# An RWKV-5 attention with a gated mixture of experts: 96 instead of 128 rows loaded per item, and half of the decayed r of six items moved from GpSimd to VectorE

## The chip, the cores and the metric

The kernel runs on one core of one Trainium2 chip. The core has five engines that run their own instruction streams: TensorE (PE, with weight loads listed as PEld), VectorE (DVE), ScalarE (ACT), GpSimd (POOL) and SyncE (SP, which here only issues transfers). 16 DMA engines move data between HBM and the on-chip memory. The metric is the device time of one execution in microseconds; 377.44 us is the median of three runs of the kernel before (376.11 to 377.89).

## The reference

Two blocks in a row. The attention keeps a 48 by 48 state per batch and head, decayed by `w` at each of 768 steps; the second block routes each token to one of eight experts.

```python
B, H, S, D = 4, 8, 768, 48
for t in range(S):
    cur = einsum('bhd,bhe->bhde', u * k[:, :, t], v[:, :, t])
    y[:, :, t] = einsum('bhd,bhde->bhe', r[:, :, t], state + cur)
    state = w[:, :, None] * state + einsum('bhd,bhe->bhde', k[:, :, t], v[:, :, t])
x = y, heads side by side            # (4, 768, 384)
e = argmax(x @ w_gate), or the expert of the token before where sigmoid(x @ w_local) >= 0.5
out = softmax(x @ w_gate)[e] * (relu(x @ w1[e]) @ w2[e])   # 8 experts, 384 -> 1024 -> 384
```

## The kernel before

**Items.** The attention runs over 16 items, one per batch and pair of heads, item n in `Attention.run`'s loop of 17 turns. An item's two heads lie on rows (partitions) 0 to 47 and 64 to 111 of a 128-row tile; rows 48 to 63 and 112 to 127 are zeros that the host put into the arrays. The 768 steps are cut into 6 chunks (`NCH`) of 128. Inside a chunk the recurrence becomes matrix products; between chunks a state is carried.

**Loads.** `load(n)` issues three transfers on SP: rk (r and k by feature, 1536 numbers a row; item 0's in two parts), kv (k and v by token) and vT (v by feature, 768 numbers a row). There are four buffers for rk and for vT (`AHEAD`) and five for kv, and `load(n + 3)` stands at the head of turn n. Eight semaphores serve these transfers in turn, so that each waits until the eighth before it has landed.

**Steps of an item.** With the lines of the profile:

- POOL, `scale(n)`, one turn ahead of PE: pd = r times k (L217, two halves of 384), ke = k by token with the decays to the chunk's end (L213), rw = r times powers of w (`decayed`, L230, two halves, for n above 2). The order is rw, ke, pd except for the first items (pd, ke) and item 4 (ke, rw, pd).
- DVE, `keys(n)`: kw = k times the inverse powers of w (L237; in two halves for items 0 to 2). For items 0 to 2 DVE makes rw as well, interleaved with kw, from a copy of the powers (`first`) that ACT puts into PSUM tile mp; `inv`, kw's factor, is also in PSUM. `reciprocals(i)` (L156, L157) makes `inv` of head pair i by a Newton step on DVE.
- PE: scores of kw and rw (L291, two groups into two PSUM banks, `pair`), which DVE masks into am (L293, two of 768); own (L268), the u term from pd, which DVE multiplies with vT (L276, y); added (L249), the chunk sums from ke and v into mp, which DVE's scan turns into the states S (L255); inside (L300), am times v; before (L313), rw times S; then ACT copies y out (L321), PE turns it (L332) and ACT stores it into x (L334). After the last item of a batch come the logits (L345, L346, L351, L352).

The banks `pair` alternate: every score group, turn or logits product takes the other one and has to wait until its last reader is done.

**Order.** The Tile framework runs with a manual schedule: each engine takes its instructions in the order in which the program is written, and `run` is that order. In turns 1 and 2 PE does scores, own and added of item n behind inside and before of item n − 1. From turn 4 on the scores run one item ahead, and kw two items ahead of that turn (turn 4 makes kw of items 4, 5 and 6, turn n makes that of n + 2). From turn 5 on DVE's order in a turn is: first am, y, kw, second am, scan.

**Constants.** `__init__` builds `tab`, a table of the powers of w and of 1/w (L121 to L132; head pair 0 on DVE, the rest on POOL), and `step`, factors for the scan (L117). `warm` and `align` are PE transposes without a use of their result. The router behind the attention needs iotas from POOL (`numbering`, in turn 2) and casts of them from ACT (`cast`, in turn 6); its own steps lie between the attention's on DVE, such as L709, L741 and L806. Expert 0's weights are fetched in the last turns, and from about 110 us on the experts run, which the change does not touch.

## Time and profile before

| | |
|---|---|
| median of three runs | 377.44 us |
| the profiled execution | 379.17 us |
| its span, first to last instruction | 377.5 us |
| mean granted TensorE clock | 0.996 |
| busy: PE, DVE, ACT, POOL | 363.0, 247.7, 110.3, 148.7 us |
| read from HBM | 64.79 MB |

The profile's page gives each engine's busy time, then the span in 40 slices of 9.4 us: a digit is the busy share of a slice in tenths, and the row DMA is the mean share of the 16 DMA engines. A row of the timeline has start, duration, engine, source line, operation, output and inputs, shape, count (neighbours of one kind are merged, so that x2 with 1.82 us are two operations), and in brackets how long the engine stood idle before and what ended that idle time. In the list of groups a row ends with the group's busy time and the mean ns of one. Times of PE operations overlap, because matmuls are pipelined; a busy PE may be waiting inside. "Issue" stands for time in which nothing shown was waited for. Where the engine named as the end of a wait had long been done, the wait was for something else, often a transfer.

### The profile page before, as it was taken

How to read it: one execution, taken by the hardware profiler on the slowest of the kernel's cores; microseconds unless marked ns; L12 is line 12 of the kernel's file. 1: busy time of each engine (PE TensorE's matmuls, PEld its weight loads, DVE VectorE, ACT ScalarE, POOL GpSimd, SP SyncE). 2: the span in 40 equal slices, each digit the busy share in tenths (PEclk: the TensorE clock that was granted, in tenths of full speed). 3: DMA queues.
4: the chain of work that ended last, by engine and by line, in shares of the span. 5: the costliest groups of instructions: out<-in, count | busy, mean ns of one | idle time of the engine just before them, and what ended most of it. 6: DMA issues, size and time to landing. Idle time of an engine off the chain costs nothing. (4 is left out here: it accounts for less than half of the span.)

```text
span 377.5 us, 9676 instructions
## 1 busy us (share of the span) xinstructions
PE 363.0 (96%) x3844; PEld 319.6 (85%) x3844; DVE 247.7 (66%) x718; ACT 110.3 (29%) x304; POOL 148.7 (39%) x207
## 2 busy tenths in 40 slices
PE   7899999999989999999999999999999999999992
PEld 6676777786769998999899999999999998989971
DVE  6988778888834835787557656857767767555300
ACT  4132233233532211322332233333243233331210
POOL 7689999786222055212333113313233023021012
PEclk9999999999999999999999999999999999999998
DMA  7999999983669457713352452164165065162011
GB/s 245 417 411 410 407 405 338 370 300 109 196 232 340 160 188 296 299 27 115 140 198 62 147 214 87 49 218 190 38 207 213 22 215 206 21 257 112 2 41 38
DMA packets 17765, 74.93 MB, mean 199 GB/s; under 512 B 2778, under 2 KB 6624, under 8 KB 15408
## 3 DMA queue, kind: packets, MB, share of 16 engines
q1 hardware_dynamic: 10336, 56.89, 40.7%
q0 software_dynamic: 3424, 9.48, 7.4%
q10 hardware_dynamic: 3952, 7.87, 5.7%
q8 instruction: 32, 0.52, 0.6%
q14 instruction: 21, 0.17, 0.1%
HBM read 64.79 MB, written 9.47 MB: 197 GB/s over the span
## 5 line engine op out<-in xcount | busy, mean ns | idle before, releaser
L1333 POOL DMA_INDIRECT out_dram<-yo,sid x27 | 26.6, 985 | 115.5 <-ACT yo L1328 92.0
L1184 PE MATMUL h<-exT,w1t 128*128 128x168 f32 (+4 forms) x240 | 54.9, 327 | 0.0
L1188 DVE TENSOR_TENSOR hT<-h,hs 128x168 f32<-128x168 f32 (+3 forms) x60 | 21.1, 351 | 46.1 <-PE h L1184 29.6
L1107 POOL DMA_INDIRECT xg<-x_d,gid x29 | 31.1, 1072 | 34.1 <-DVE gid L877 15.1
L1184 PEld LDWEIGHTS h<-exT,w1t 128*128 128x128 f32 x240 | 41.6, 190 | 0.3 <-issue 0.3
L1134 PE MATMUL h<-exT,w1t 128*128 128x168 f32 (+2 forms) x192 | 37.2, 333 | 0.5 <-DVE lt L698 0.5
L1253 PE MATMUL y<-factors,sums 128*128 128x192 f32 x168 | 36.8, 326 | 0.0
L293 DVE TENSOR_TENSOR am<-pair,kept 128x768 f32<-128x768 f32 x32 | 30.0, 953 | 8.9 <-PE pair L291 8.4
L217 POOL TENSOR_TENSOR pd<-rk 128x384 f32<-128x384 f32 x32 | 31.5, 1006 | 10.6 <-PE y L268 10.0
L1184 PE MATMUL h<-xs,ws 128*128 128x168 f32 (+4 forms) x144 | 35.3, 327 | 0.0
L1134 PEld LDWEIGHTS h<-exT,w1t 128*128 128x128 f32 x192 | 30.9, 190 | 2.6 <-DVE lt L698 0.6
L1184 PEld LDWEIGHTS h<-xs,ws 128*128 128x128 f32 x144 | 25.5, 190 | 4.3 <-ACT hs L1191 1.2
L1253 PEld LDWEIGHTS y<-factors,sums 128*128 128x128 f32 x168 | 28.9, 190 | 0.2
L291 PE MATMUL pair<-rw,kw 48*64 48x128 f32 (+1 forms) x768 | 23.4, 249 | 1.9 <-issue 1.1
L300 PE MATMUL y<-am,kv 128*64 128x128 f32 x360 | 22.9, 276 | 1.3 <-DVE y L276 1.2
L230 POOL TENSOR_TENSOR rw<-rk,tab 128x384 f32<-128x384 f32 x26 | 23.7, 936 | 0.4 <-DMA rk<-in_rk_dram 0.4
L1121 DVE COPY exT<-tp 128x384 f32<-128x384 f32 (+5 forms) x29 | 13.9, 485 | 14.7 <-PE tp L1120 14.6
L291 PEld LDWEIGHTS pair<-rw,kw 48*64 48x64 f32 x768 | 19.6, 133 | 4.6 <-issue 2.8
L1253 PE MATMUL y<-w2t,hT 128*128 128x192 f32 x96 | 23.0, 328 | 0.0
L213 POOL TENSOR_TENSOR ke<-kv,endT 128x288 f32<-128x288 f32 (+1 forms) x32 | 21.9, 705 | 1.9 <-DMA kv<-in_kv_dram 1.0
L321 ACT COPY xT<-y 128x768 f32<-128x768 f32 x15 | 12.0, 800 | 33.1 <-PE y L313 31.1
L300 PEld LDWEIGHTS y<-am,kv 128*64 128x64 f32 x360 | 19.4, 137 | 2.4 <-DVE y L276 1.7
(298 smaller groups left out, 736.6 us busy)
## 6 DMA issues: line engine op xcount, KB each, us to landing
w1t<-in_w_dram SPq DMA_DIRECT2D x8, 1536.0 KB, 6.9
w2t<-in_w_dram SPq DMA_DIRECT2D x8, 1536.0 KB
rk<-in_rk_dram SPq DMA_DIRECT2D x15, 768.0 KB, 8.4
kv<-in_kv_dram SPq DMA_DIRECT2D x16, 584.0 KB, 7.1
vT<-in_vT_dram SPq DMA_DIRECT2D x16, 384.0 KB
x_d<-x ACTq DMA_DIRECT2D x4, 1152.0 KB
w1t<-in_w_dram SPq DMA_DIRECT2D x2, 768.0 KB
w2t<-in_w_dram SPq DMA_DIRECT2D x2, 768.0 KB
```

The costliest lines, as they stand in the source:

```text
L213: nc.gpsimd.tensor_mul(t["ke"][:, z], t["k"][:, z], spread(self.endT[:, p, hp], 1, len(range(NCH)[z])))
L217: nc.gpsimd.tensor_mul(t["pd"][:, z], t["rT"][:, z], t["kT"][:, z])
L230: engine.tensor_mul(t["rw"][:, z], t["rT"][:, z], spread(pw, 1, z.stop - z.start))
L291: nc.tensor.matmul(sc[f * DP:(f + 1) * DP, h, i, x:], lhsT=t["kw"][q, c, o * DP:(o + 1) * DP], rhs=t["rw"][q, c, x:], start=True, stop=True)
L293: return lambda: nc.vector.tensor_mul(t["am"][:, g], sc, spread(self.kept[:, g:g + 3], 1, 2))
L300: nc.tensor.matmul(t["y"][h][p * DP:(p + 1) * DP, c2 * P:(c2 + 1) * P], lhsT=t["v"][:, (2 * c + h) * DH:(2 * c + h) * DH + DP], rhs=t["am" ...
L1107: self.nc.gpsimd.indirect_dma_start(out=xg[:n], out_offset=None, in_=self.x_d[:rows], in_offset=bass.IndirectOffsetOnAxis(ap=u["gid"][:n, ...
L1134: nc.tensor.matmul(h[:, :n], lhsT=u["w1"][:, m, kk, :], rhs=u["xT"][:, kk, :], start=(kk == 0), stop=(kk == DK - 1))
L1184: nc.tensor.matmul(out, lhsT=a, rhs=b, start=start and k == 0, stop=stop and k == len(terms) - 1, skip_group_check=True)
L1188: nc.vector.tensor_tensor(out, a, b, op=Alu.add)
L1253: return lambda: nc.tensor.matmul(bank[:, x * half:(x + 1) * half], lhsT=a, rhs=b, start=(j == 0 and x == 0), stop=(j == FK // 2 - 1), ski ...
L1333: self.nc.gpsimd.indirect_dma_start(out=out.rearrange("n (h d) -> (n h) d", h=2) if half else out, out_offset=bass.IndirectOffsetOnAxis(ap ...
```

## The change

1. **Loads.** rk comes as two transfers of 48 rows (0 to 47 and 64 to 111) for all items but 0 and 3, and vT likewise for all but items 0, 2 and 3. The zeros in the other rows stay in a buffer from one item to the next. Buffers that get no whole load first are cleared on the chip: rk buffer 1 by a DVE memset, vT buffer 1 and rk buffer 2 by three ACT copies of 768 zeros from step. These stand ahead of the loads in the program. For item 4 kv is issued ahead of rk.
2. **Decayed r.** For items 3 to 8 POOL makes the first half of rw and DVE the second, behind kw, with the factor from tab in SBUF. For item 2 DVE makes the first half and POOL the second.
3. **Reciprocals of head pair 1.** `inverse(1)`, three operations on POOL and an ACT copy into `inv`, takes the place of `reciprocals(1)` on DVE, and the three warming transposes ahead of it on PE go.
4. **Numbering.** The iotas move from turn 2 to turn 8, ahead of `scale(9)`, and the casts from turn 6 to turn 8.

```diff
+SHARED = range(3, 9)
...
+        self.step = once.tile([P, HP, DH, NCH - 1], F32, name="step")
+        nc.vector.memset(self.step, 0.0)
+        nc.vector.memset(self.rks[1], 0.0)
+        zero = self.step.rearrange("p i d c -> p (i d c)")[:, :NCH * P]
+        for t in (self.vTs[1], self.rks[2]):
+            t = t.rearrange("p a c t -> p (a c t)")
+            for x in range(0, t.shape[1], NCH * P):
+                nc.scalar.copy(t[:, x:x + NCH * P], zero)
         for i in range(AHEAD - 1):
             self.load(i)
...
+    def inverse(self, i):
+        nc, w, inv = self.nc, self.tab[:, i, 0, 1:], self.tab[:, i, 1, 1:]
+        nc.gpsimd.tensor_mul(self.more, w, inv)
+        nc.gpsimd.tensor_scalar(self.more, self.more, -1.0, 2.0, Alu.mult, Alu.add)
+        nc.gpsimd.tensor_mul(self.more, self.more, inv)
+        nc.scalar.copy(self.inv[:, i], self.more)
...
+        whole, parts = (slice(0, P),), (slice(0, DH), slice(DP, DP + DH))
+        rows = whole if n in (0, AHEAD - 1) else parts
+        src = self.rk_d[b, hp].rearrange("p (a c t) -> p a c t", a=2, c=NCH)
+        if n == AHEAD:
+            nc.sync.dma_start(out=kv, in_=self.kv_d[b, hp])
+        for z in (slice(0, NCH),) if n else (slice(0, C2), slice(C2, NCH)):
+            for q in rows:
+                nc.sync.dma_start(out=rk[q, :, z], in_=src[q, :, z])
+        if n != AHEAD:
+            nc.sync.dma_start(out=kv, in_=self.kv_d[b, hp])
+        for q in whole if n < AHEAD and n != 1 else parts:
+            nc.sync.dma_start(out=vT[q].rearrange("p a c t -> p (a c t)"), in_=self.vT_d[b, hp][q])
...
         def rw(i):
-            self.decayed(nc.gpsimd, n, slice(i * C2, (i + 1) * C2))
+            if i == 0 or n not in SHARED:
+                self.decayed(nc.gpsimd, n, slice(i * C2, (i + 1) * C2))
+        if n == 2:
+            rw(1)
...
-        pw = self.first[:, :P] if n < 3 else self.tab[:, t["hp"], 0, :P]
+        pw = self.first[:, :P] if n < 3 and engine is self.nc.vector else self.tab[:, t["hp"], 0, :P]
...
-            if n < 3:
+            if n < 2 or n == 2 and z.start == 0:
                 self.decayed(nc.vector, n, z)
+        if n in SHARED:
+            self.decayed(nc.vector, n, slice(C2, NCH))
...
-                self.warm(3)
+                self.inverse(1)
                 self.added(0)
-                self.reciprocals(1)
                 self.states(0)
                 self.scale(1)
...
-                else:
-                    router.numbering()
...
+            if n == HP * 2:
+                router.numbering()
             if n + 1 < M:
                 self.scale(n + 1)
...
-            if n == 6:
+            if n == HP * 2:
                 router.cast()
```

How the streams move, at the places that the prediction speaks of. First DVE from the powers of item 3 to the first am of item 5 in the program before (rk_160 is the buffer of item 3, rk_157 that of item 4, rk_158 that of item 5; tab and mp hold the powers):

```order
L157 SCALAR_TENSOR_TENSOR inv<-mp,tab 128x128
L237 TENSOR_TENSOR kw<-rk_160,inv 128x768
L660 MEMSET r_ones 128x128
L255 SCALAR_TENSOR_TENSOR S<-step,mp 128x240
L293 TENSOR_TENSOR am<-pair_152,kept 128x768
L293 TENSOR_TENSOR am<-pair_151,kept 128x768
L276 TENSOR_TENSOR y<-y,vT_164 128x2x384
L237 TENSOR_TENSOR kw<-rk_157,inv 128x768
L255 SCALAR_TENSOR_TENSOR S<-step,mp 128x240
L237 TENSOR_TENSOR kw<-rk_158,inv 128x768
L293 TENSOR_TENSOR am<-pair_151,kept 128x768
```

And the same stretch of DVE in the changed program:

```order
L265 TENSOR_TENSOR kw<-rk_160,inv 128x768
L257 TENSOR_TENSOR rw<-rk_160,tab 128x384
L689 MEMSET r_ones 128x128
L285 SCALAR_TENSOR_TENSOR S<-step,mp 128x240
L323 TENSOR_TENSOR am<-pair_151,kept 128x768
L323 TENSOR_TENSOR am<-pair_152,kept 128x768
L306 TENSOR_TENSOR y<-y,vT_164 128x2x384
L265 TENSOR_TENSOR kw<-rk_157,inv 128x768
L257 TENSOR_TENSOR rw<-rk_157,tab 128x384
L285 SCALAR_TENSOR_TENSOR S<-step,mp 128x240
L265 TENSOR_TENSOR kw<-rk_158,inv 128x768
L257 TENSOR_TENSOR rw<-rk_158,tab 128x384
```

One rw of 384 stands behind each kw: one ahead of the scan of item 3, two ahead of am of item 4.

POOL in the same part of the program before, from the last two of the iotas of `numbering` to pd of item 4 (rk_157; kv_168 and kv_169 hold items 3 and 4):

```order
L636 IOTA tie_i 128x6
L636 IOTA ief_i 1x8
L230 TENSOR_TENSOR rw<-rk_160,tab 128x384 x2
L213 TENSOR_TENSOR ke<-kv_168,endT 128x3x96
L213 TENSOR_TENSOR ke<-kv_168,endT 128x2x96
L217 TENSOR_TENSOR pd<-rk_160 128x384 x2
L213 TENSOR_TENSOR ke<-kv_169,endT 128x3x96
L213 TENSOR_TENSOR ke<-kv_169,endT 128x2x96
L230 TENSOR_TENSOR rw<-rk_157,tab 128x384 x2
L217 TENSOR_TENSOR pd<-rk_157 128x384 x2
```

And in the changed program, from the end of item 2's ke to the same pd:

```order
L232 TENSOR_TENSOR ke<-kv_167,endT 128x2x96
L257 TENSOR_TENSOR rw<-rk_160,tab 128x384
L232 TENSOR_TENSOR ke<-kv_168,endT 128x3x96
L232 TENSOR_TENSOR ke<-kv_168,endT 128x2x96
L236 TENSOR_TENSOR pd<-rk_160 128x384 x2
L232 TENSOR_TENSOR ke<-kv_169,endT 128x3x96
L232 TENSOR_TENSOR ke<-kv_169,endT 128x2x96
L257 TENSOR_TENSOR rw<-rk_157,tab 128x384
L236 TENSOR_TENSOR pd<-rk_157 128x384 x2
```

The iotas are gone from here and rw is one half instead of two. On DVE around item 7 (rk_160 now holds item 7) the rows between y of item 5 and the scan read, changed:

```order
L323 TENSOR_TENSOR am<-pair_151,kept 128x768
L306 TENSOR_TENSOR y<-y,vT_162 128x2x384
L265 TENSOR_TENSOR kw<-rk_160,inv 128x768
L257 TENSOR_TENSOR rw<-rk_160,tab 128x384
L323 TENSOR_TENSOR am<-pair_152,kept 128x768
L285 SCALAR_TENSOR_TENSOR S<-step,mp 128x240
```

Before, kw is followed by the second am there.

More of the change, by code (lines that the diff above doesn't have):

```diff
@@ L113, in __init__ @@
         nc.sync.dma_start(out=self.wp, in_=wp_d)
-        self.step = once.tile([P, HP, DH, NCH - 1], F32, name="step")
-        nc.vector.memset(self.step, 0.0)
         self.tab = tab = once.tile([P, HP, 2, P + 1], F32, name="tab")
@@ L133, in __init__ @@
             n += m
+        self.more = once.tile([P, P], F32, name="more")
         self.first, self.newton = mp[:, :P + 1], mp[:, P + 1:2 * P + 1]
@@ L192, in load @@
         rk, vT, kv = self.rks[n % AHEAD], self.vTs[n % AHEAD], self.kvs[n % (AHEAD + 1)]
-        if n:
-            nc.sync.dma_start(out=rk.rearrange("p a c t -> p (a c t)"), in_=self.rk_d[b, hp])
-        else:
-            for z in (slice(0, C2), slice(C2, NCH)):
-                nc.sync.dma_start(out=rk[:, :, z], in_=self.rk_d[b, hp].rearrange("p (a c t) -> p a c t", a=2, c=NCH)[:, :, z])
-        nc.sync.dma_start(out=kv, in_=self.kv_d[b, hp])
-        nc.sync.dma_start(out=vT.rearrange("p a c t -> p (a c t)"), in_=self.vT_d[b, hp])
+        whole, parts = (slice(0, P),), (slice(0, DH), slice(DP, DP + DH))
[10 more added lines that the diff above has]
+            nc.sync.dma_start(out=vT[q].rearrange("p a c t -> p (a c t)"), in_=self.vT_d[b, hp][q])
         self.items[n].update(b=b, hp=hp, rT=rk[:, 0], kT=rk[:, 1], vT=vT,
@@ L207, in scale @@
         t["pd"] = self.two.tile([P, NCH, P], F32, name="pd")
-        t["rw"] = self.four.tile([P, NCH, P], F32, name="rw")
+        self.room(n)
         hp = t["hp"]
@@ L225, in scale, with room @@
                 what(i)
+    def room(self, n):
+        t = self.items[n]
+        if "rw" not in t:
+            t["rw"] = self.four.tile([P, NCH, P], F32, name="rw")
     def decayed(self, engine, n, z):
         t = self.items[n]
-        pw = self.first[:, :P] if n < 3 else self.tab[:, t["hp"], 0, :P]
+        pw = self.first[:, :P] if n < 3 and engine is self.nc.vector else self.tab[:, t["hp"], 0, :P]
         engine.tensor_mul(t["rw"][:, z], t["rT"][:, z], spread(pw, 1, z.stop - z.start))
@@ L234, in keys @@
         t["kw"] = self.two.tile([P, NCH, P], F32, name="kw")
+        self.room(n)
         inv = self.inv[:, t["hp"]]
@@ L400, in run @@
                     self.reciprocals(2)
-                else:
-                    router.numbering()
                 self.scale(n + 1)
```

## The prediction

> **What bounds the kernel now.** I read the page first, then the busy time by stretches, then who waited for whom, then the timeline of the attention half. The page's span and slices (40 of 9.4 us):
>
> ```profile
> span 377.5 us, 9676 instructions
> ...
> DMA  7999999983669457713352452164165065162011
> GB/s 245 417 411 410 407 405 338 370 300 109 196 232 340 160 188 296 299 27 115 140 198 62 147 214 87 49 218 190 38 207 213 22 215 206 21 257 112 2 41 38
> ```
>
> The change touches only the attention half, up to about 110 us. There the DMA engines are full for six slices at about 410 GB/s, and the change takes bytes from them and work from GpSimd (POOL). But do these two set the pace? Two stretches by engine (columns PE, PEld, DVE, ACT, POOL, clock, DMA share, GB/s):
>
> ```profile
> 10.00:20.00 10.00, 8.95 (x191) 7.08 (x191) 9.11 (x17) 1.71 (x3) 7.04 (x9) 1.00 1.02 411
> 50.00:60.00 10.00, 9.98 (x238) 7.99 (x234) 7.71 (x10) 2.86 (x9) 9.34 (x12) 1.00 1.01 393
> ```
>
> Early, VectorE (DVE) is the fullest of the compute engines (9.11) and TensorE (PE) has gaps (8.95); later PE has none (9.98), and POOL at 9.34 looks as if it were short. Who waits for loads? In the table of waits up to 110 us (total, times, longest) only POOL waits for rk or kv, three times; two of the rows, and the third as it stands in the timeline:
>
> ```profile
> POOL ke L213 <- DMA kv<-in_kv_dram: 1.0, 1, 1.0
> POOL pd L217 <- DMA rk<-in_rk_dram: 0.4, 1, 0.4
> ```
>
> ```profile
> 21.37 1.69 POOL L230 TENSOR_TENSOR rw<-rk,tab 128x384 f32<-128x384 f32 x2 [0.42 <-DMA rk<-in_rk_dram]
> ```
>
> That is rw of item 3, and PE reads it 6 us later (the scan ahead of that item's am, quoted below, starts at 27.80). What PE waits for is DVE. Items 0 and 1, in order of time:
>
> ```profile
> 10.64 0.96 DVE L276 TENSOR_TENSOR y<-y,vT 128x768 f32<-128x768 f32 x1
> ...
> 10.87 0.49 PE L163 MATMUL pair<-ident 128*128 128x128 f32 x3
> ...
> 11.29 0.79 PE L249 MATMUL mp<-kv,ke 128*64 128x48 f32 x20
> ...
> 11.91 1.50 PE L300 MATMUL y<-am,kv 128*64 128x128 f32 x24
> 12.22 0.30 DVE L156 SCALAR_TENSOR_TENSOR mp<-mp,tab 128x128 f32<-128x128 f32 x1 [0.63 <-PE mp L249]
> ...
> 12.77 0.64 DVE L255 TENSOR_TENSOR_SCAN S<-step,mp 128x240 f32<-128x240 f32 x1
> 13.32 0.53 DVE L237 TENSOR_TENSOR kw<-rk,inv 128x384 f32<-128x384 f32 x1
> 13.46 0.90 PE L313 MATMUL y<-rw,S 48*48 48x128 f32 x20
> ...
> 13.77 0.55 DVE L230 TENSOR_TENSOR rw<-rk,mp 128x384 f32<-128x384 f32 x1
> ...
> 15.37 1.82 DVE L293 TENSOR_TENSOR am<-pair,kept 128x768 f32<-128x768 f32 x2
> 17.11 0.96 DVE L276 TENSOR_TENSOR y<-y,vT 128x768 f32<-128x768 f32 x1
> 18.12 1.53 PE L300 MATMUL y<-am,kv 128*64 128x128 f32 x24 [0.82 <-DVE y L276]
> ```
>
> So the first items are a chain PE scores, DVE am twice, DVE y, PE L300 and L313, PE scores; the last row says it, 0.82 of PE's idle time ended by y, and y stands directly behind am, am directly behind DVE's four kw and rw operations, which start 0.46 apart from 13.32 on. A load or a POOL operation that is done earlier does not shorten this chain; only what stands ahead of a link on DVE or PE does.
>
> **The start, and items 0 to 2.** Cost first: DVE clears rk buffer 1 (1536 elements a row) behind step, and ScalarE (ACT) writes zeros three times 768.
>
> ```profile
> 1.09 0.86 DVE L117 MEMSET step<- 128x960 f32 x1 [1.09 <-PEq L1770]
> 3.19 0.17 DVE L124 TENSOR_SCALAR w<-w_t 128x4 f32<-128x4 f32 x1 [1.23 <-DMA w_t<-in_wu_dram]
> 5.72 0.27 ACT L136 COPY mp<-tab 128x129 f32<-128x129 f32 x1 [3.13 <-DVE tab L132]
> ```
>
> 960 elements take 0.86 us, so 1536 take 1.37; DVE sat idle 1.23 us at that place, so the chain that starts at L124 is 0.14 late. ACT had 3.13 us free; three copies at about 0.8 (estimated from kw's 0.53 for 384 and am's 0.91 for 768) take 2.5 and cost nothing. The loads of items 1 and 2 wait for these writes, behind item 0's transfers that fill the DMA engines anyway.
>
> Gain: PE's three warming transposes (10.87 to 11.29) and DVE's two operations from 12.22 to 12.77 go. L300 of item 0 then starts when y is done: 10.64 + 0.96 + 0.14 + 0.05 = 11.79 instead of 11.91. The scan, which had ended at 13.41 and so held L313, can follow y and L249 at about 11.9 and be over at 12.6; L313 then stands behind L300's 1.50 alone, at 13.29 for 13.46: 0.17 gained on PE. DVE comes to kw of item 1 at about 12.6 for 13.32, 0.7 earlier. am needs both, the scores of PE and a free DVE, so L300 of item 1 gains between 0.17 and 0.7; I take 0.27, near PE's end, as DVE is now ahead. POOL's three operations in their stead (about 1.1 us by POOL's 0.94 for 384 elements and its start-up, between ke of item 0 and pd of item 1) lie under DVE's y and scan, and ACT's copy behind them under the scan; if POOL or ACT were over 0.3 late with them, kw would wait and the gain be gone. The half of item 2's rw that POOL makes instead of DVE gives nothing: from scores of item 2 on PE and am set the chain. **Sum so far −0.27 us.**
>
> The iotas move from behind item 2, where POOL waited 0.42 for rk afterwards, to behind pd of item 8, and ACT's casts with them to just ahead of the logits of that item. POOL's products are an item ahead there (below), so 0; if the casts held up ACT's copies, whose bank PE needs, it would be one cast group, at most 0.5 by ACT's 0.27 an operation.
>
> **Items 3 to 8: half of rw on DVE.** Six operations more, each 13.77 − 13.32 = 0.46 us of DVE. They differ from rw of items 0 to 2 in one point: the factor comes from tab in SBUF, not from mp in PSUM. What such a form costs beside POOL:
>
> ```profile
> 70.71 1.97 POOL L230 TENSOR_TENSOR rw<-rk,tab 128x384 f32<-128x384 f32 x2
> ...
> 71.81 0.89 DVE L709 SCALAR_TENSOR_TENSOR key<-lt,k 128x12 f32<-128x12 f32 x1
> ```
>
> ```profile
> L806 DVE SCALAR_TENSOR_TENSOR si<-r,eb 128x12 int32<-128x12 f32 x1 | 0.2, 172 | 0.0
> ```
>
> The same shape takes 0.17 us with POOL at rest and 0.89 here, ending at 72.70, when POOL's second half ends (72.68): a DVE operation with two SBUF inputs waits until POOL's running one is through. The wait lies between 0 and one POOL operation, 0.94:
>
> ```profile
> L230 POOL TENSOR_TENSOR rw<-rk,tab 128x384 f32<-128x384 f32 x26 | 23.7, 936 | 0.4 <-DMA rk<-in_rk_dram 0.4
> ```
>
> I take half of it times POOL's load after the change (about 0.8), 0.37. What DVE has to give, at the places concerned:
>
> ```profile
> 27.80 0.65 DVE L255 TENSOR_TENSOR_SCAN S<-step,mp 128x240 f32<-128x240 f32 x1 [0.70 <-PE mp L249]
> ...
> 34.66 1.82 DVE L293 TENSOR_TENSOR am<-pair,kept 128x768 f32<-128x768 f32 x2 [1.17 <-PE pair L291]
> ```
>
> Item 3: 0.46 + 0.37 against 0.70 of idle before the scan, 0.13 over. Items 4 and 5, both ahead of am of item 4: 1.66 against 1.17, 0.49 over; L345 and the scores of item 5 wait for that am's bank. Item 6 falls in a longer gap: 0. Items 7 and 8 stand between y and the second am, and PE's next scores need the bank that this am empties:
>
> ```profile
> 45.43 1.97 POOL L217 TENSOR_TENSOR pd<-rk 128x384 f32<-128x384 f32 x2
> 46.26 0.94 DVE L237 TENSOR_TENSOR kw<-rk,inv 128x768 f32<-128x768 f32 x1
> 47.12 0.95 DVE L293 TENSOR_TENSOR am<-pair,kept 128x768 f32<-128x768 f32 x1
> ...
> 48.43 0.28 PE L291 MATMUL pair<-rw,kw 48*64 48x128 f32 x2
> ...
> 52.44 0.95 DVE L293 TENSOR_TENSOR am<-pair,kept 128x768 f32<-128x768 f32 x1
> ...
> 53.89 0.27 PE L291 MATMUL pair<-rw,kw 48*64 48x128 f32 x2
> ```
>
> am ends at 48.07, the scores start at 48.43: 0.36 spare. For item 8 am ends at 53.39 and the scores start at 53.89: 0.50 spare. kw ends 0.20 before pd there, so the wait is 0.2: 0.66 − 0.36 = 0.30 and 0.66 − 0.50 = 0.16. **Sum 0.13 + 0.49 + 0.30 + 0.16 = +1.08.** With no wait at all only 0.10 stays; with 0.94 each time it is 0.70 + 1.63 + 1.04 + 0.90 = 4.27. POOL's lighter load itself buys nothing: pd of item 7 ends at 47.40, and PE reads it behind the scores of item 8, 6 us later.
>
> **The loads.** rk and vT now come as two transfers of 48 rows:
>
> ```profile
> rk<-in_rk_dram SPq DMA_DIRECT2D x15, 768.0 KB, 8.4
> kv<-in_kv_dram SPq DMA_DIRECT2D x16, 584.0 KB, 7.1
> vT<-in_vT_dram SPq DMA_DIRECT2D x16, 384.0 KB
> ```
>
> At 411 GB/s these take 1.91, 1.46 and 0.96 us, 4.33 an item. If time goes by bytes, an item's load falls to 0.75 × 2.87 + 1.46 = 3.61 and all comes earlier; as no DVE or PE operation waits for a load, that is worth 0. The trace of before has no load that covers part of the rows, so the other end is a rival below. [...]
>
> **Sum.** −0.27 + 1.08 + 0 = +0.8 us. The profiled execution took 379.17 us, its span 377.50 and 1.67 around it; the median of the three runs is 377.44, below it by 1.73, so I put the difference on both: 380.0 for such a profiled run, 378.2 for the median. About 0.5%, 1.9 us, is what a measurement of this kernel tells from no change.
>
> **Rivals.** *DVE's extra work is hidden* (15%): POOL, with half of rw gone, stands idle when DVE asks, and the waits are 0: −0.27 + 0.10, 377.3. For it: POOL waits for PE before later pd. Against: pd and kw start together, as quoted. *Faster* (13%): PE's early gaps are due to late data after all, through waits that the trace books on other engines, and earlier loads close them. From L313 of item 0 at 13.46 to the scores of item 8 at 53.89 are 40.4 us; six items at the pace of the last (53.89 − 48.43 = 5.46) would be 32.8. The other 7.6 hold one batch's logits, one set of scores made ahead, and the gaps of the first four items; if a third came back, it would be 2.4: 375.0. For it: DMA is full and POOL at 9.34 in this stretch. Against: the chain above names DVE and PE alone. *Slower through the loads* (19%): a transfer's time follows the rows at its fullest target, not its bytes. Point of decision, rk of item 5 for DVE's kw:
>
> ```profile
> 32.56 0.93 DVE L237 TENSOR_TENSOR kw<-rk,inv 128x768 f32<-128x768 f32 x1
> ...
> 95.48 0.94 DVE L237 TENSOR_TENSOR kw<-rk,inv 128x768 f32<-128x768 f32 x1
> ```
>
> At half speed, rk takes 2.88 and vT 1.44, 5.8 us an item. Before, the transfers up to rk of item 3 add up to 3 × 4.33 + 0.3 (wp) + 1.91 = 15.2, and POOL's wait for it ended at 21.37, 6.1 later. After, items 0 to 3 take 4.33 + 5.78 + 5.3 + 4.33 and 0.3 for wp, item 4 5.78 and rk of item 5 2.88: 28.7, landing at 34.8, 2.2 after 32.56. The idle 1.17 before am covers what the added rw leave of it, say 0.7: +1.5, with DVE's extra work 380. If each half takes as long as the whole, an item takes 7.2 us, the loads add up to 109, rk of item 15 lands at about 112 and kw wants it at 95.5: +16, 394. For it: no load of before covers part of the rows, so nothing rules it out. Against: 48 rows are fewer bytes, and every load of before ran at the rate of its bytes. [...]
>
> **How the numbers follow.** Forecast 50%, own range 377.3 to 381.4 (the two ends of DVE's wait). Hidden 15%, faster 13%, loads slower 19%, of which half about 380 and half about 394; 3% for what I have not seen. The range 375.3 to 381.4 leaves out the worst of the loads and a part of faster. Faster by over 0.5%: 13% and 2% of the rest. Slower: the forecast's upper part from 379.3 on (13%), and the loads' 17%. Same: 55%.
>
> **What would show it.** Right: L313 of item 1 near 19.3; the six new rw on DVE above 0.55 us where POOL runs, the am of item 4 at about 35 and a later scores row of items 7 and 8; rk landing earlier than before; POOL with gaps from 36 us on. Wrong: the new rw at 0.55 each, waits of DVE kw for rk, a DMA share still at 1.0 beyond 75 us, or L313 of item 4 well before 42.

## The result and the profile after

The changed kernel takes 401.81 us in the median of six runs (398.99 to 404.74), the kernel before 377.65 in six runs beside it (376.11 to 378.84): a ratio of 1.0634, 95% interval 1.0575 to 1.0692. That is 24 us slower, where +0.8 was forecast and the range ended at 381.4. The profiled execution of after (398.99, span 397.3) is the fastest of the six; against the span before it lost 19.8 us. Executions over 1.5% above the fastest of their kernel (one of 945 us in run 3, two in run 10, one in run 17) are left out of the times and ratios below.

The page of after, with the same lines as before and the granted clock (40 slices, now of 9.9 us):

```profile
span 397.3 us, 9734 instructions
...
PEclk9996996988899999999999999999999999999997
DMA  7999979979978665690345245146146145054011
GB/s 229 282 333 232 239 235 209 231 214 246 216 206 288 231 274 200 218 369 29 94 153 189 72 171 199 44 150 224 62 150 252 50 158 212 30 191 181 2 39 35
```

Read DMA and GB/s together. Before, the DMA engines were full for seven slices and moved 405 to 417 GB/s in the first five of them. Now they are full, or nearly, up to the thirteenth slice and from the fourth to the twelfth move 206 to 246. The program reads 4 MB less and the engines are busy for longer: that is no shortage of bytes but of rate. Two stretches, as shown of before, and one more (PE, PEld, DVE, ACT, POOL, clock, DMA share, GB/s):

```profile
10.00:20.00 10.00, 8.34 (x174) 6.35 (x168) 8.28 (x14) 1.92 (x4) 6.26 (x10) 1.00 1.02 284
...
50.00:60.00 10.00, 9.07 (x200) 7.29 (x196) 7.79 (x10) 2.49 (x6) 4.60 (x5) 1.00 0.76 232
60.00:70.00 10.00, 8.94 (x162) 7.18 (x164) 5.78 (x8) 1.64 (x4) 7.84 (x18) 0.66 1.04 209
```

From 50 to 70 PE had no gap before; now it has, and from 60 to 70 it is granted 0.66 of its clock. The waits up to 110 us name what was absent before (before, only POOL waited for rk or kv, three times, 0.4 to 1.0 us each):

```profile
POOL rw L257 <- DMA rk<-in_rk_dram: 12.5, 10, 2.6
POOL ke L232 <- DMA kv<-in_kv_dram: 9.0, 10, 1.7
DVE kw L265 <- DMA rk<-in_rk_dram: 2.9, 4, 1.3
```

The DMA queue of the loads, first before and then after (packets, MB, share of 16 engines over the span):

```profile
q1 hardware_dynamic: 10336, 56.89, 40.7%
```

```profile
q1 hardware_dynamic: 9904, 52.86, 44.8%
...
kv<-in_kv_dram SPq DMA_DIRECT2D x16, 584.0 KB, 10.7
rk<-in_rk_dram SPq DMA_DIRECT2D x28, 288.0 KB, 9.7
```

40.7% of 377.5 us are 153.6 us of the queue's time, 44.8% of 397.3 are 178.0: 24.4 us more for 4 MB less. The halves are 28 of rk (288 KB) and 26 of vT (144 KB), 12.1 MB; whole they would be 16.1 MB, 39.2 us at 411 GB/s. If all of the time more is put down to the halves, they took about 63.6 us, which is 190 GB/s, and a half of rk took 1.55 us where the whole one takes 1.91. This reckoning (queue time beyond 153.6 us) is used for each experiment below.

It charges the halves with more than their own time. The trace also has a record of every packet, and a packet's size tells its tensor: a row of rk has 6144 bytes, one of vT 3072, one of kv 4672. Mean times of a packet over items 4 to 15, and the queue's time for an item:

| | before | after |
|---|---|---|
| a row of rk | 249 ns | 460 ns |
| a row of vT | 136 ns | 201 ns |
| a row of kv | 184 ns | 300 ns |
| an item: rk + vT + kv | 1.99 + 1.09 + 1.47 = 4.55 us | 2.76 + 1.21 + 2.40 = 6.36 us |

kv comes whole, in 128 rows, in both kernels, and about half of the queue's extra time (12.6 us of the 24.4) is kv's. So a half is not only slow itself: the whole loads that stand in the queue with it become slow too. The rates of the reckoning are the price of such halves, not their own speed.

### The profile page after: what moved, and what is told of

The parts are those of the page before. It is cut to its first block, busy times and chain, and to the rows that moved or that the text cites. A ratio compares the mean times of both kernels' runs of the same rounds, so it can differ in the third digit from the quotient of the medians.

```text
span 397.3 us, 9734 instructions
## 1 busy us (share of the span) xinstructions
PE 375.4 (95%) x3841; PEld 327.6 (82%) x3841; DVE 254.1 (64%) x722; ACT 112.7 (28%) x308; POOL 145.8 (37%) x205
## 3 DMA queue, kind: packets, MB, share of 16 engines
q1 hardware_dynamic: 9904, 52.86, 44.8%
## 5 line engine op out<-in xcount | busy, mean ns | idle before, releaser
L257 POOL TENSOR_TENSOR rw<-rk,tab 128x384 f32<-128x384 f32 x21 | 19.2, 930 | 23.8 <-DMA rk<-in_rk_dram 13.6
L330 PE MATMUL y<-am,kv 128*64 128x128 f32 x360 | 27.0, 308 | 0.7 <-DVE y L306 0.7
L330 PEld LDWEIGHTS y<-am,kv 128*64 128x64 f32 x360 | 23.6, 159 | 1.7 <-DVE y L306 1.1
```

The lines of the kernel that those rows point to most:

```text
L257: engine.tensor_mul(t["rw"][:, z], t["rT"][:, z], spread(pw, 1, z.stop - z.start))
L330: nc.tensor.matmul(t["y"][h][p * DP:(p + 1) * DP, c2 * P:(c2 + 1) * P], lhsT=t["v"][:, (2 * c + h) * DH:(2 * c + h) * DH + DP], rhs=t["am" ...
```

## The experiments

Theories. **R**: a transfer of fewer rows is slow, and the loads set the pace. **N**: it is the number of transfers, five an item for three, on semaphore lanes that they share. **V**: VectorE's halves of rw. Ratios are against the kernel before, run beside each. The cuts of code show the loop over rk; vT is cut in the same way.

**1. Whole loads, the rest of the change kept.**

```diff
-        rows = whole if n in (0, AHEAD - 1) else parts
+        rows = whole
...
-        for q in whole if n < AHEAD and n != 1 else parts:
+        for q in whole:
```

> The changed kernel with every rk and vT loaded whole (128 rows, one transfer) again; the clears, the DVE halves of rw and the changed start stay. Theory R (rows: a transfer of 48 rows moves at about half the rate of one of 128, so the loads supply the attention too slowly): 378 to 379 us, DMA busy share down from 1.0 as in the kernel before, GB/s back to about 400 in the first 20 us. Theory N (number: five transfers an item instead of three, on eight shared lanes): also 378 to 379. Theory V (the loss is made by VectorE's halves of rw, which hold the pipeline up through the wait behind GpSimd): 395 to 402. This run also prices all of the change but its loads: my forecast of those parts was +0.8 us.

Measured: 378.19 us, ratio 0.9988 (0.9965 to 1.0011). The loss is gone with the halves, V falls, and all else in the change is worth −0.5 us (−1.3 to +0.4), where my steps gave +0.8.

```profile
DMA  7999999992669457713352452164165065072011
GB/s 244 415 411 410 405 389 317 343 368 90 206 239 356 154 191 307 289 39 124 121 198 62 164 215 70 54 229 178 37 208 217 16 218 204 20 260 111 3 42 36
```

Both rows are those of the kernel before again. The start, which the late loads hide in the changed kernel, can be read here: PE's L330 of item 1 and DVE's first kw of item 1 (18.12 and 13.32 in the rows of before):

```profile
17.70 1.53 PE L330 MATMUL y<-am,kv 128*64 128x128 f32 x24 [0.70 <-DVE y L306]
```

```profile
12.71 0.53 DVE L265 TENSOR_TENSOR kw<-rk,inv 128x384 f32<-128x384 f32 x1
```

**2. The loads and their clears alone, in the kernel before** (the changed `load` and the clears, nothing else).

> The kernel before with the change's loads and clears alone (48-row halves, VectorE's memset, ScalarE's clearing copies), no DVE halves of rw and the old start. Theories R and N: 397 to 402 us, granted clock near 0.96, GB/s 210 to 250 in the slices up to 120 us. Theory V: 376 to 380.

Measured: 400.44, ratio 1.0572 (1.0539 to 1.0605). With run 1 this closes the account: within the intervals the loads are all of the loss.

**3. and 4. The number of transfers against their shape.** Both keep five transfers an item and all bytes; one cuts rows, one cuts columns.

```diff
-            nc.sync.dma_start(out=rk.rearrange("p a c t -> p (a c t)"), in_=self.rk_d[b, hp])
+            for q in (slice(0, P),) if n == AHEAD - 1 else (slice(0, DP), slice(DP, P)):
+                nc.sync.dma_start(out=rk[q].rearrange("p a c t -> p (a c t)"), in_=self.rk_d[b, hp][q])
...
```

```diff
+            src, k = rk.rearrange("p a c t -> p (a c t)"), NCH * P
+            for z in (slice(0, 2 * k),) if n == AHEAD - 1 else (slice(0, k), slice(k, 2 * k)):
+                nc.sync.dma_start(out=src[:, z], in_=self.rk_d[b, hp][:, z])
...
```

> The kernel before with the same number of transfers as the change, but each half holds 64 rows (0 to 63, 64 to 127), so all of the bytes move (64.8 MB instead of 60.8). Theory R: slow, and slower than the change as the bytes are a third more per half: 400 to 420 us. Theory N: 397 to 404. If 48 rows are bad by their number (three rows for each of 16 DMA engines) and 64 are not: 377 to 380.

> The kernel before with the same number of transfers as the change, all bytes, but each rk and vT is cut by columns: two transfers of all 128 rows with half as many bytes in a row. Theory R: 377 to 380 us, GB/s as in the kernel before. Theory N: 397 to 404 us.

Measured: rows 413.03, ratio 1.091 (1.0874 to 1.0947); columns 377.78, ratio 0.9974 (0.9944 to 1.0005). GB/s by rows and by columns:

```profile
GB/s 226 226 315 224 220 276 195 242 233 206 246 265 313 279 250 218 213 291 271 32 172 141 126 39 180 200 41 184 205 36 240 164 102 249 36 165 194 2 38 34
```

```profile
GB/s 249 410 402 397 392 396 352 344 333 105 210 234 349 168 196 322 273 38 125 119 198 62 159 218 72 57 227 176 36 208 216 19 217 205 20 262 111 2 42 37
```

N falls for five transfers an item. A half of 64 rows is slow too (about 211 GB/s by the reckoning; a row of rk takes 420 ns, one of kv 291), and as it holds a third more bytes than one of 48, it costs more.

**5. 64 rows two apart.** The same halves, but the even rows and the odd rows.

```diff
+            for q in (slice(0, P),) if n == AHEAD - 1 else (slice(0, P, 2), slice(1, P, 2)):
...
```

> The kernel before with the halves of the third run cut another way: rk and vT each come in two transfers of 64 rows, the even rows and the odd ones, so that each transfer writes to both ends of the 128 partitions. Bytes, count and length of a row are those of the halves 0 to 63 and 64 to 127, which made 413.8 us. Theory P (what is slow is a transfer that lies in one half of the partitions): 377 to 381 us, GB/s about 400 up to 65 us. Theory Q (a transfer of 64 rows is slow because it has few rows for the 16 DMA engines, wherever they lie): 405 to 420 us, GB/s 210 to 250.

Measured: 379.62, ratio 1.0056 (1.0038 to 1.0074), q1 at

```profile
q1 hardware_dynamic: 10768, 56.89, 40.6%
```

of 377.8 us, 153.4: as the kernel before, and a row of rk takes 255 ns, one of kv 187. The 2 us that it lost are small beside the 34 of run 3. So it is not that 64 rows are few; it is where they lie. This pair of runs (3 and 5), equal in count, bytes and row length, settles it for 64 rows: the halves that lie in one half of the partitions are slow (420 ns a row of rk for 255).

**6. and 10. Rows 0 to 111 and rows 0 to 119 in one transfer** (items 4 to 15).

```diff
+            for q in (slice(0, P if n < AHEAD else DP + DH),):
...
```

> The kernel before with one transfer of rows 0 to 111 for each rk and vT of items 4 to 15 (the 16 rows at the end were loaded as zeros with items 0 to 3 and stay so). 14.2 MB of rk and vT become 12.4 MB. Theory P: the lower 64 rows still set the time of a transfer, so each takes as long as the whole one (1.9 us for rk) and the share of q1 stays near 40%; the time 377 to 379 us. Theory Q, and going by bytes: each transfer takes 12.5% less, 3 us less of q1's 154 us; the time the same, since TensorE sets the pace. Both 376 to 379 us; the queue's time tells them apart.

> The kernel before with one transfer of rows 0 to 119 for each rk and vT of items 4 to 15. Rows 0 to 111 made 396.6 us, all 128 377.8. Theory S (what matters is how the rows fall to the DMA engines: 120 rows are 15 shares of 8, as 128 are 16 of 8, where 112 are 16 of 7 that lie across each other): 377 to 381 us, q1's time near that of the kernel before. Rival (any transfer short of all 128 rows is slow): 390 to 400 us.

Measured: 396.56, ratio 1.0493 (1.0476 to 1.0511), and for run 10 398.71 and 402.5 in two executions, too few for an interval. Both theories of run 6 had 376 to 379, and the theory of shares of eight rows had 377 to 381 for run 10: all wrong. The rival of run 10 (any transfer short of all 128 rows is slow, 390 to 400) had the direction and about the size. The queue:

```profile
q1 hardware_dynamic: 9952, 55.12, 43.0%
```

```profile
q1 hardware_dynamic: 10120, 56.00, 43.5%
```

169.8 and 174.3 us of queue time: by the reckoning 112 rows go at about 245 GB/s, 120 at 241. By the packets a row of rk takes 372 and 378 ns, so rk of 112 rows takes 2.6 us, longer than the whole rk (1.99 by its packets); kv's rows take 267 and 275.

**7. Lower halves on SyncE's queue, upper halves on ScalarE's** (64 rows, items 4 to 15).

```diff
+            for k, q in enumerate((slice(0, P),) if n < AHEAD else (slice(0, DP), slice(DP, P))):
+                (nc.scalar if k else nc.sync).dma_start(out=rk[q].rearrange("p a c t -> p (a c t)"), in_=self.rk_d[b, hp][q])
...
```

> The kernel before with rk and vT of items 4 to 15 in halves of 64 rows, the lower half issued by SyncE and the upper by ScalarE's queue, so that a lower and an upper half can be in flight together. Theory P: with both halves under way at once the rate comes back to about 400 GB/s wherever both queues have work; 380 to 395 us, what is over 378 being ScalarE's waits for free buffers. Theory Q: as slow as halves on one queue, 400 to 414 us, GB/s 210 to 250.

Measured: 411.31, ratio 1.0886 (1.0861 to 1.0911), 216 to 225 GB/s from 30 to 60 us. A second queue did not bring the halves together: on one queue, in run 3, the ratio was 1.091.

**8. VectorE's halves of rw alone, in the kernel before.**

```diff
+            if i == 0 or n not in SHARED:
+                self.decayed(nc.gpsimd, n, slice(i * C2, (i + 1) * C2))
...
+        if n in SHARED:
+            self.decayed(nc.vector, n, slice(C2, NCH))
```

> The kernel before with one edit of the change alone: VectorE makes the second half of rw of items 3 to 8 after kw. My forecast of that step: +1.1 us (0.1 to 4.3), which was 0.46 us an item at first plus a wait for GpSimd's running operation. The rival (hidden behind other waits): within 0.3 us of the kernel before. The first run, which held this edit and the changed start, gave a ratio of 0.9988, so I now expect 0.997 to 1.002.

Measured: 378.11, ratio 1.0003 (0.9983 to 1.0024), which is +0.1 us (−0.6 to +0.9). Two of the six operations, and PE at the scores of item 8, behind them and at its next gap:

```profile
33.97 1.27 DVE L237 TENSOR_TENSOR rw<-rk,tab 128x384 f32<-128x384 f32 x1
...
47.23 0.70 DVE L237 TENSOR_TENSOR rw<-rk,tab 128x384 f32<-128x384 f32 x1
```

```profile
54.40 1.24 PE L301 MATMUL pair<-rw,kw 48*64 48x128 f32 x48
...
58.89 0.79 PE L323 MATMUL y<-rw,S 48*48 48x128 f32 x18
...
79.64 0.21 PE L301 MATMUL pair<-rw,kw 48*64 48x64 f32 x1 [0.21 <-issue]
```

The six take 0.55, 0.76, 1.27, 1.25, 0.70 and 0.70: waits of 0 to 0.7 behind POOL, 0.32 on average (0.15 at items 7 and 8), about as forecast. The scores of item 8 start late, at 54.40 instead of 53.89, but the products ahead of the scores of item 9 are only 0.24 late (58.89). Two rows of the kernel before:

```profile
58.65 0.79 PE L313 MATMUL y<-rw,S 48*48 48x128 f32 x18
...
85.72 0.21 PE L291 MATMUL pair<-rw,kw 48*64 48x64 f32 x1 [0.84 <-issue]
```

The gap of 0.84 there is missing in this run, whose only one nearby is the 0.21 at 79.64, an item earlier. So the little that was late is taken up, and attention ends no later.

**9. and 12. Does the lower clock cost time?** In the changed kernel PE waits 1.83 us, and this follows:

```profile
30.75 1.37 PE L321 MATMUL pair<-rw,kw 48*64 48x128 f32 x38 [1.83 <-issue]
...
31.91 1.67 PE L298 MATMUL y<-pd,w_t 48*64 48x384 f32 x7
...
35.66 2.67 PE L330 MATMUL y<-am,kv 128*64 128x128 f32 x24
```

L330 took 1.53 before; the clock that was granted from 32 to 38 is 0.50 (columns as in the stretches above):

```profile
32.00:38.00 6.00, 6.00 (x63) 4.54 (x57) 5.51 (x8) 0.70 (x2) 3.77 (x4) 0.50 1.03 234
```

Run 9 fills PE's gaps in the changed kernel with spare transposes, run 12 puts four gaps into the kernel before (a transpose that waits for two copies of ScalarE).

```diff
+                self.fill(FILL)
                 self.scores(ahead, 0)()
...
+                self.fill(FILL)
                 self.own(n)
```

```diff
             self.before(n - 1)
+            if n in GAPS:
+                h = 2 * self.items[n - 1]["hp"]
+                self.nc.scalar.copy(self.pause, self.xTs[(n - 1) // HP].rearrange("p h x -> p (h x)")[:, h * C2 * P:h * C2 * P + 512])
+                self.nc.scalar.copy(self.pause[:, :256], self.pause[:, 256:])
+                self.nc.tensor.transpose(self.pairs[1][:, 0, 3 * P:], self.pause[:, :P], self.ident)
```

> The changed kernel with two spare 128x128 transposes on TensorE ahead of the scores and two ahead of own(n) of items 3 to 15 (about 1.1 us of extra TensorE work an item, into columns of the score banks that nothing reads), so that TensorE's waits for late rows are partly filled. Theory K (in the changed kernel each gap of TensorE of 1.4 us or more is followed by some 6 us at half the granted clock, and that costs time on top of the late rows): fewer slices of PEclk under 9 and 392 to 399 us, although work was added. Rival (the rows alone set the pace, the lower clock lies beside the waits): 402 to 408 us, since the added work can only lengthen.

> The kernel before with four gaps put into TensorE's stream by hand: ahead of the scores in the steps of items 6, 8, 10 and 12 a transpose waits for two extra copies on ScalarE (about 2 us after the last product of the item before). No load is touched. Rival (a gap costs its own length): 4 times 2 us and the four transposes, 384 to 387 us, PEclk 9 throughout. Theory K: each gap is followed by about 6 us at half clock, in which TensorE's work takes some 2 to 3 us longer: 392 to 398 us, with dips in PEclk between 45 and 110 us.

Measured: run 9 404.95, ratio 1.0698 (1.065 to 1.0745); run 12 391.34, ratio 1.0325 (1.0275 to 1.0374). One of the four gaps of run 12, and the stretches behind it:

```profile
64.77 0.33 PE L445 MATMUL pair<-ident,pause 128*128 128x128 f32 x1 [1.99 <-ACT pause L444]
```

```profile
66.00:68.00 2.00, 2.00 (x28) 0.78 (x24) 1.77 (x3) 0.00 (x0) 0.01 (x1) 0.50 0.31 116
68.00:70.00 2.00, 2.00 (x17) 0.50 (x10) 1.75 (x2) 0.00 (x0) 2.00 (x3) 0.69 0.10 12
70.00:72.00 2.00, 2.00 (x35) 1.64 (x37) 0.67 (x2) 1.18 (x3) 2.00 (x3) 1.00 0.96 329
```

Four gaps and transposes are 4 × (1.98 + 0.33) = 9.2 us; the run lost 12.3 by the ratio (10.4 to 14.1), so something added about 0.8 us a gap, between 0.3 and 1.2. The half clock behind each gap is the likely cause; that the two extra copies on ScalarE add nothing was not tested. Theory K had 2 to 3: the lower clock is there, its price was smaller. Run 9 lifted the mean clock from 0.965 to 0.977 and did not win, as its rival had it, but it decides nothing. Its rows in a stretch at full clock:

```profile
87.58 0.44 PE L182 MATMUL pair<-ident 128*128 128x128 f32 x2
...
89.81 0.44 PE L182 MATMUL pair<-ident 128*128 128x128 f32 x2 [0.63 <-DVE am L328]
...
94.49 0.44 PE L182 MATMUL pair<-ident 128*128 128x128 f32 x2
```

An item takes 6.91 us there (87.58 to 94.49) without PE or DVE waiting for a load: the spare work, and its own wait of 0.63 for a score bank, set PE's pace.

**13. and 14. The stores of x off the loads' lanes.** After the first store is issued at 45.80, SyncE can't issue a load; the rows give start and length of its issues:

```profile
45.32 9.67 SPq L214 DMA_DIRECT2D rk<-in_rk_dram  x2
55.08 0.38 SPq L216 DMA_DIRECT2D kv<-in_kv_dram  x1
```

```profile
SPq L214 <- DMA x_d<-x: 18.2, 2, 9.1
```

and the DMA engines run dry (two stretches, columns as above):

```profile
52.00:56.00 4.00, 3.41 (x92) 2.53 (x88) 3.57 (x5) 0.80 (x1) 2.12 (x2) 1.00 0.38 119
82.00:86.00 4.00, 4.00 (x45) 3.34 (x44) 3.38 (x7) 0.70 (x2) 3.26 (x4) 0.57 0.38 140
```

The edit gives the stores of the first two sequences to GpSimd, one step later, in the changed kernel (13) and in the kernel before (14).

```diff
+            if b > 1:
+                self.store(nc.scalar, b)
...
+            if n in (HP + 2, 2 * HP + 2):
+                self.store(self.nc.gpsimd, n // HP - 1)
```

> The changed kernel with the stores of x of the first two sequences issued by GpSimd one step later, so that SyncE's loads no longer wait for a lane behind them (18.2 us of such waits in the changed kernel, two of 9.1 us, with the DMA engines empty for some 5 us behind them). If those holes are on the path: 3 to 6 us faster than the change, 396 to 399. If the slow halves alone set the end, since the queue only drains later: 400 to 403.

> The same move of the two stores in the kernel before, as the control: there the loads are ahead of TensorE, so 377 to 380 either way.

Measured: 405.0, ratio 1.0701 (1.0631 to 1.0772), and 384.84, ratio 1.0204 (1.016 to 1.0248). The control failed: it lost 7.5 us by itself, most of it in one new gap,

```profile
79.74 0.84 PE L249 MATMUL mp<-kv,ke 128*48 128x48 f32 x20 [4.45 <-POOL rw L230]
```

and the trace shows where it comes from:

```profile
73.02 5.24 DVE L714 TENSOR_TENSOR k<-t,k 128x12 f32<-128x12 f32 x1
```

The store's issue keeps GpSimd from 72.10 to 73.00; then its own operations follow one another without a gap until 79.81. DVE's small operation, with two inputs in SBUF, took 0.17 us before (at 71.61); here it starts with GpSimd's first one and is held for 5.24. DVE's scan stands behind it and ends at 79.64, and L249, which overwrites what the scan reads, follows at 79.74. So here VectorE waited behind GpSimd far longer (5.24 us for 0.17) than one GpSimd operation of 0.94, which the prediction took as the wait's upper end.

In the changed kernel the edit lost about 2.5 against the change, within the two intervals, and the same operation was held for 2.74. That would fit holes worth some 5 us, but an edit with such a cost shows neither; it stays open.

**15. to 18. Which rows are slow?** Items 4 to 15: 48 rows two apart (0 to 94 and 1 to 95), rows 0 to 95 at once, rows 0 to 31, 32 to 95 and 96 to 127 apart, and 32 rows four apart; one line of each, in this order.

```diff
+            for q in (slice(0, P),) if n < AHEAD else (slice(0, 96, 2), slice(1, 96, 2)):
...
+            for q in (slice(0, P if n < AHEAD else 96),):
...
+            for q in (slice(0, P),) if n < AHEAD else (slice(0, 32), slice(32, 96), slice(96, P)):
...
+            for q in (slice(0, P),) if n < AHEAD else [slice(i, P, 4) for i in range(4)]:
```

> The kernel before with rk and vT of items 4 to 15 in two transfers of 48 rows each, rows 0, 2, ... 94 and rows 1, 3, ... 95; rows 96 to 111 are left as they were, so a part of the heads' last rows is computed from other items' data. Count, bytes and row length are those of the change's halves. Theory P (where the rows lie): at about 400 GB/s the halves take 0.7 us for rk, and the time is 376 to 381. Theory Q (48 rows are too few or fall badly on 16 DMA engines): q1 as slow as with the change, 392 to 402.

> The kernel before with one transfer of rows 0 to 95 for each rk and vT of items 4 to 15 (rows 96 to 111 left as they were, as in the run beside it): the same bytes as the 48-row pairs, consecutive rows, one transfer. Rows 0 to 111 and 0 to 119 went at about 240 GB/s. If consecutive rows short of all 128 go at that rate, 590 KB of rk take 2.5 us: 386 to 398. If 96 rows go by bytes as all 128 do: 376 to 380.

> The kernel before with rk and vT of items 4 to 15 in three transfers: rows 0 to 31, 32 to 95 and 96 to 127, all bytes. The middle one is 64 consecutive rows, 32 of the lower and 32 of the upper half. Rule E (a transfer is fast when its rows fall evenly on both halves of the partitions): only the outer 64 rows are slow, q1 takes some 18 us longer than in the kernel before (154 us) and the time is 382 to 395. Rule R (consecutive rows short of all 128 are slow, rows at an even step over all 128 are fast): all three are slow, q1 takes some 36 us longer, 400 to 412.

> The kernel before with rk and vT of items 4 to 15 in four transfers of 32 rows each, four apart (0, 4, ... 124 and so on), all bytes, nine transfers an item. Rules E and R: as fast as 64 rows two apart (379.6), 377 to 386, the more so as SyncE has nine issues an item to make; q1's time near 154 us. If 64 rows two apart were fast only because 64 rows are enough: slow, 395 to 420.

In runs 15 and 16 what follows attention works on other data and takes over 2 ms, so only the loads' stretch is read, here 48 rows two apart and then rows 0 to 95:

```profile
40.00:50.00 10.00, 9.67 (x202) 6.78 (x199) 6.97 (x28) 1.98 (x4) 7.55 (x9) 1.00 1.03 235
```

```profile
40.00:50.00 10.00, 6.73 (x107) 4.22 (x101) 5.89 (x9) 1.18 (x3) 7.45 (x10) 0.88 1.02 226
```

The kernel before moves about 406 there (fifth and sixth slice of its GB/s row). Both are slow, though their rows lie in both halves, two to one: theory P is not the whole rule. Run 17: 400.36, ratio 1.0627 (1.0566 to 1.0688). Run 18: 398.17, ratio 1.0518 (1.0466 to 1.057). Their queues:

```profile
q1 hardware_dynamic: 11104, 56.89, 44.2%
```

```profile
q1 hardware_dynamic: 11488, 56.89, 40.7%
```

Run 17: 44.2% of 395.9 are 175.0 us, 21.4 more than before, near the 18 of rule E, while the run's time lies at the lower end of the range of rule R. The queue's time gives only the sum. The packets decide against E's reading, by which half of the rows would be fast: only 12% of rk's rows took under 260 ns (before, 95%), and in the order in which they started the first 32 of an item took 391 ns, the next 64 371 and the last 32 365. So all three pieces were slow. Whether the middle one would be fast without the outer ones beside it stays open, since they slow kv too (256 ns a row). Run 18: 161.3 us, only 7.7 more, and half of rk's rows took 234 ns or less, as in the kernel before; it is slow for another reason, SyncE comes to issue too late:

```profile
SPq L195 <- DMA x_d<-x: 20.9, 3, 7.6
```

Nine issues an item at about 0.6 us, and three waits for a store: read from the trace, N holds here, which at five transfers didn't.

**11. What a better version could be.** Whole loads with rk in two transfers of all rows, r before k.

```diff
+        for a in (slice(0, 1), slice(1, 2)) if n else (slice(0, 2),):
```

> The changed kernel with all 128 rows, and rk of items 1 to 15 in two transfers of all rows: first r, then k. The whole loads alone gave a ratio of 0.9988, column halves in the kernel before 0.9974. If the two add up: 0.995 to 0.998; if both are nothing: 0.998 to 1.002.

Measured: 378.62, ratio 1.0019 (0.999 to 1.0048). Nothing; no version found is faster than the kernel before by more than its interval.

## Why the prediction was wrong

**The step that failed is the loads' term**: "If time goes by bytes, an item's load falls to 0.75 × 2.87 + 1.46 = 3.61 [...] that is worth 0". It is not 3.61 us but 1.46 + 2 × 1.55 + 2 × 0.78 = 6.1 by the reckoning, and 6.4 by the packets of items 4 to 15: rk 2.76, vT 1.21, and kv, which no forecast had touched, 2.40 instead of 1.46. My argument "every load of before ran at the rate of its bytes" was true and proved nothing, since every one of them held all 128 rows. The runs show about 211 GB/s for halves of 64 rows (run 3) and 190 for the change's 48, where whole loads moved 411, and no gain from a second queue (run 7). The count of packets did not decide the rate: each of the 27 added transfers added 16 packets of 4 bytes (1552 for 1120), as many as each of the 70 transfers of before has.

**The third rival put the loss where it was, in the loads, at too low a price.** It had 380 for half speed (5.8 us an item) and 394 for halves as long as the whole (7.2). Half speed was an assumption that no run shows as such: by the reckoning the halves went at 0.46 of the whole loads' rate (190 for 411 GB/s). Nor does a run show the rival's rule that a transfer's time follows the rows at its fullest target; what they show is that rk of 112 rows took 2.6 us, longer than the whole one's 1.99 (run 6). At half speed it priced rk at 2.88 and vT at 1.44, a little more than the packets give; what it left out is that kv becomes slow as well. The measured item lies near the first price, yet the loss is that of the second and more. That the second had rk of item 15 landing at about 112, as it came, was luck: it got there with 7.2 us an item. By my own sum with 6.1, rk of item 15 would land at about 97 (4.33 + 6.1 + 5.5 + 4.33 + 0.3 + 12 × 6.1 − 3.0 = 90.8, and 6.1 for the way); its last half was issued at 102.4, its last packet ended at 111.4, and POOL's rw waited for it until 112.73. kw of item 15, at 95.48 before, ran at 116.16:

```profile
112.73 1.68 POOL L257 TENSOR_TENSOR rw<-rk,tab 128x384 f32<-128x384 f32 x2 [1.15 <-DMA rk<-in_rk_dram]
...
116.16 0.94 DVE L265 TENSOR_TENSOR kw<-rk,inv 128x768 f32<-128x768 f32 x1
```

What I had left out, as an estimate from the rows above: two stores of x of 1.18 MB that stand in the same engines' time (2.9 us each), two stretches of 4 us at a share of 0.38 behind SyncE's waits for lanes (5), and kv and halves together moving 235 GB/s rather than what 6.1 asks for (2). That is 13 of the 15; 2 are not placed. From the landing to kw it is 4 us more; no idle time of DVE stands ahead of kw there, it follows am and y of the items before in DVE's order. These parts are read from the trace and not shown by an experiment; the sum of them, the loads' loss, is (runs 1 and 2).

**DVE's halves of rw** (+1.08): the waits were about right, the term was not. Run 8 has +0.1 (−0.6 to +0.9): a late start of the scores was mostly made up within the item, 0.24 stayed behind item 8, and a later gap took that up. I had added four delays as if PE had no slack behind any of them. The rival "hidden" had the time, for another reason than its own, since the waits were there: luck too. The upper end of the wait, one GpSimd operation, is no bound (5.24 us in run 14).

**The start** (−0.27): run 1 has L330 of item 1 0.42 earlier (17.70 for 18.12) and kw of item 1 at 12.71, forecast at about 12.6. The mechanism is as forecast, a little larger, and its gain fits the −0.5 of that run; in the changed kernel the late rk of items 1 and 2 ate it.

**What would show it**: DVE's kw waiting for rk and a DMA share of 1.0 beyond 75 us were named as signs of being wrong, and both came. Of the signs of being right, the new rw above 0.55 us came (five of six in run 8).

## What to carry to other kernels

Here a load's price went by how its rows lay in the memory, not by its bytes alone (a row of rk took 255 ns as one of 64 two apart and 420 in rows 0 to 63 and 64 to 127), a badly placed one slowed the whole loads beside it (300 ns a row of kv for 184), and a trace in which every transfer held all 128 rows said nothing about one that doesn't. Cut by columns, the transfers lost nothing (377.78 us in run 4, 413.03 by rows in run 3); to leave out rows of padding cost more than it saved, even 8 rows of 128 (398.71 in run 10). In another kernel, try both before trusting the bytes, and look at GB/s beside the DMA share: full engines at about half their former rate were the sign (232 GB/s at a share of 1.02 from 30 to 40 us, 408 at 1.02 before).

## What the runs showed of the hardware

- A row of rk (6144 bytes) took, in the mean of items 4 to 15: 249 ns as part of all 128 rows, 255 as one of 64 rows two apart, 301 as one of 32 rows four apart (234 in the median, as before). Slow: 460 in the change's 48-row halves, 420 in rows 0 to 63 and 64 to 127, 372 in rows 0 to 111, 378 in rows 0 to 119, 397 in rows 0 to 95, 393 in 48 rows two apart, 375 in the three pieces of run 17. So only transfers whose rows are spread evenly over all 128 were fast; that even 120 of 128 rows lose was expected by the rival of run 10 alone. The cause is open.
- While such slow transfers are in the queue, whole loads are slow too: a row of kv took 300 ns in the changed kernel and 291 in run 3, for 184 before and 187 in run 5.
- A gap of TensorE of 1.4 to 2.8 us went with 3.4 or 6.8 us at half the granted clock (by the clock's records up to 110 us, four times in the changed kernel and four in run 12; 0.50 from 32 to 38 us of after, behind a gap of 1.83), and about 0.8 us beyond the gap itself was lost (run 12).
- A store on ScalarE's queue stopped SyncE's loads for 9.1 us, twice; run 13, with these stores on GpSimd, has no such wait. That semaphore lanes shared by both queues are the way is the likely reading, not shown apart.
- A VectorE operation with two inputs in SBUF was held for 5.24 us, 0.17 before, while GpSimd worked without a gap (run 14).
